# A two-layer MLP on split fp32: the scheme of seven for one more pair of chunks, other staging, output sums in two groups

## Chip, cores and metric

One core of a Trainium2 chip. The metric is the device time of one execution of the whole program in microseconds. An execution of the same program under the profiler gives the trace.

## What is computed

The reference takes x of 2 x 3008 x 256, applies a spectral layer (a Fourier transform along the sequence, a complex 256 x 256 product, soft thresholding, the inverse transform) and then two MLP layers on the 6016 tokens:

```python
h = x @ w_in                                  # 256 -> 2048
x = (h * sigmoid(1.702 * h)) @ w_out          # layer 0, 2048 -> 256
h = x @ w_in2
x = (h * sigmoid(h)) @ w_out2                 # layer 1
```

Only layer 1 and the preparation of its weights during layer 0 are touched by the change. The inputs and outputs are fp32.

## The kernel before, in words

Tokens lie along the free dimension, features along the 128 partitions. The tokens are cut into six blocks; blocks 0 to 4 have two halves of 512 tokens, block 5 has two halves of 448. The 2048 hidden features are cut into eight pairs p of two chunks of 128. A **stage** (l, i, p) is layer l, block i, pair p: its products from x to the hidden features, their activation, and the products to the output. Every fp32 operand is split into a high part and a low part, and one block product is three matmuls (high x high, high x low, low x high).

The products from x to the hidden features of a stage are 2 x 2 blocks, made with seven block products and sums on the operands (`prod`, 21 matmuls). The products to the output are made one stage later than the stage whose factors they use: the standard way with eight block products, 24 matmuls (`out_mm` in layer 0, `out7` in layer 1, called through a list `pend`), or with a scheme of seven block products, 21 matmuls (`s_prod`, called through `S`). `seven(i)` lists the p that use the scheme of seven in layer 1: 1 to 5. Stages with p from 1 to 6 of layer 1 run through `group7`, all others through `group`. In `group7` the factors of a g7 stage are: y1 (factor 1), y4 (2), b22 (3), t1 (5), t2 (6), t3 (7), t4 (4), where t1 = y3 - y1, t3 = b22 - y3, t2 = b22 - t1, t4 = t2 - y4. ScalarE gates and rounds the high parts, GpSimd and VectorE subtract the low parts (`rest`, L1208). The low part of factor 3 is made by ScalarE's negative copy and an accumulating DMA from GpSimd's queue (L1251) that reads b22; the gate of b22 in the next stage overwrites b22.

Sums of products stay in PSUM banks m1, m2, m6, m7 and m3 over a block (`banks`), those of factors 4 and 5 are added into SBUF by VectorE (`accs`). In p = 6 these are combined (`ends`) in u1, u2, a5, a6, and after p = 7 four sums `final` add a bank and an SBUF part, and SyncE copies the result out (L1160, L1162). The weights of the scheme of seven are sums and splits that are made during layer 0 (`stage`, six steps at places given by STEPS, or LATE in block 5), written to DRAM, and loaded in layer 1 by `stream` into the two slots of `ring`, 1 MB a stage. Before that each unit of layer 1's weights is converted from 64-bit input during layer 0 (`window`, in the order of WEIGHTS) and written to DRAM. `halve` stages the weights of the two pairs that stay standard.

The order of all instructions on each engine is that of the program: the regions of the MLP are scheduled by hand, and `hook(h)` marks eight places in a stage at which side work is put in. `xsums`, `xfifth` and `xprep` make the seven operands of the next block from its x (L883, L884, L888, L898, L905). ScalarE copies y1, y2 and y3 out of PSUM, VectorE adds the second product; a product that accumulates on a bank (`first=False`) waits until that copy is done.

The lines the text refers to: L1009 and L1191 products from x, L968 and L1150 standard products to the output, L1127 products of the scheme of seven, L1039 and L1219 first add of a stage, L1069, L1074, L1244, L1246 second and third add, L272 low split in `stage`, L1286 two sums in p = 7, L1110 load of the ring.

Of the kernel before, what the change touches and what calls it, by code (L numbers as in the profile page):

```python
# [34 lines left out]
WEIGHTS += [(kind, 1, p, False) for kind in ("in", "out") for p in range(8)]  # L35
# [21 lines left out]
def spectral_mlp_kernel(ctx, tc, xin, mfwd, minv, wc, bias, w_in1, w_out1, w_in2, w_out2, outT):  # L57
# [938 lines left out]
    def group(l, i, p, hook):  # L996
# [37 lines left out]
        (nc.vector.tensor_copy if (l, i, p) == (1, 0, 0) else nc.scalar.copy)(y1, X)  # L1034
# [142 lines left out]
    def group7(i, p, hook):  # L1177
# [37 lines left out]
        nc.scalar.copy(y1, X)  # L1215
# [9 lines left out]
        if ends:  # L1225
            u1, u2 = (home[x][:, :n] for x in ("b22", "u"))
# [34 lines left out]
        gate(y3)  # L1261
# [13 lines left out]
        if ends:  # L1275
            add(a6, a6, a5)
            add(a5, u2, a5)
            if R3 == 1:
# [7 lines left out]
            steps7.setdefault((1, i, NPR - 1, 5), []).append(lambda: (add(a6, u2, a6), sub(u2, u2, a4)))  # L1286
# [29 lines left out]
    moves[0, last, 3].append(("out", 1, 0))  # L1316
# [284 lines left out]
```

## Time and profile before

| | us |
|---|---|
| median of 3 runs | 1124.08 (1123.69 to 1126.19) |
| profiled execution | 1127.38 |
| its span, first to last instruction | 1125.6 |

The spectral part takes the first 169 us of the span; layer 0 runs from there to 653, layer 1 to the end. A stage begins with the first matmul of its first product. The page of the profile gives the busy time of the engines, a chain of waits and the costliest groups of instructions; the trace behind it answers by stretch, by engine and by line. Stages in the tables are cut at the starts of their first matmuls.

### The profile page before, as it was taken

To read this page: it belongs to the slowest core of one execution; us is meant where nothing else is said; L and a number is where in the kernel's file an instruction comes from. 1 tells how busy PE (TensorE), PEld (TensorE's weight loads), DVE (VectorE), ACT (ScalarE), POOL (GpSimd) and SP (SyncE) were. 2 spreads that over 40 slices of the span, in tenths; PEclk is the share of its full clock that TensorE was granted. 3 is DMA by queue.
4 is the path that set the end of the run, shared out by engine and by line. 5 is a ranking of instruction groups with operands and counts; after the bars stand their busy time and mean duration, and the time that the engine had idled before them with its cause. 6 is when DMAs were issued, how large, how long until landed. Compare 5 with 4: busy or idle time off the path is not lost.

```text
span 1125.6 us, 15165 instructions
## 1 busy us (share of the span) xinstructions
PE 1117.2 (99%) x5000; PEld 928.7 (83%) x5000; DVE 839.8 (75%) x1264; ACT 831.2 (74%) x1567; POOL 584.4 (52%) x491
## 2 busy tenths in 40 slices
PE   9999999999999999999999999999999999999998
PEld 6878987888888888888889888888888888788897
DVE  8779997775575576676577687777877877878776
ACT  2488367776676677676777788878888788697785
POOL 0244056444443444434446638657657567477485
PEclk9999999999999999999999999999999999999999
DMA  8699586531121222312424263145054044242341
GB/s 334 167 169 210 151 155 121 120 73 38 38 75 38 54 60 80 108 48 84 122 94 133 84 233 100 50 160 140 10 192 117 19 151 103 74 142 57 121 138 41
DMA packets 54624, 123.87 MB, mean 110 GB/s; under 512 B 5265, under 2 KB 18193, under 8 KB 50578
## 3 DMA queue, kind: packets, MB, share of 16 engines
q1 hardware_dynamic: 36466, 92.44, 23.1%
q0 software_dynamic: 18080, 30.47, 16.9%
q8 instruction: 39, 0.64, 0.2%
q14 instruction: 39, 0.32, 0.1%
HBM read 71.85 MB, written 20.58 MB: 82 GB/s over the span
## 4 chain that ended last, share of the span: by engine, by line
PE 84%; DVE 7%; DMA 3%; issue 3%; ACT 2%; POOL 1%; SPq 0%; DVEq 0%; POOLq 0%; ACTq 0%
PE x L1009 24%; PE o L968 22%; PE x L1191 13%; PE m L1127 9%; PE m L1150 8%; PE r L1127 3%; PE y L1191 2%; PE psf L448 1%; DMA xl<-xt 1%; DMA x<-yt 1%; DMA xr<-in_x 1%; DMA cv_a<-cv_c 1%; PE psm L642 1%; PE psm L645 1%; POOL xl L567 0%
## 5 line engine op out<-in xcount | busy, mean ns | idle before, releaser
L1022 POOL TENSOR_TENSOR g<-yt,g 128x512 fp32r<-128x512 f32 (+1 forms) x174 | 234.1, 1348 | 274.4 <-PE x L1009 134.9
L1009 PE MATMUL x<-x,wi 128*128 128x512 f32 (+1 forms) x1260 | 314.8, 388 | 2.4 <-ACT yt L1059 2.3
L968 PE MATMUL o<-g,wo 128*128 128x512 f32 (+1 forms) x1152 | 280.3, 385 | 0.0
L1009 PEld LDWEIGHTS x<-x,wi 128*128 128x128 f32 x1260 | 235.3, 188 | 51.9 <-ACT yt L1059 4.9
L968 PEld LDWEIGHTS o<-g,wo 128*128 128x128 f32 x1152 | 216.3, 188 | 40.6
L1208 POOL TENSOR_TENSOR g<-yt,g 128x512 fp32r<-128x512 f32 (+1 forms) x138 | 189.4, 1388 | 74.0 <-ACT g L1204 66.5
L1012 ACT ACTIVATE yt<-yt 128x512 f32<-128x512 f32 (+1 forms) x180 | 112.0, 622 | 142.4 <-DVE yt L1069 114.5
L1191 PE MATMUL x<-x,wi 128*128 128x512 f32 (+1 forms) x648 | 167.9, 385 | 0.1
L1017 ACT CAST g<-yt 128x512 fp32r<-128x512 f32 (+1 forms) x234 | 144.0, 616 | 6.0
L1191 PEld LDWEIGHTS x<-x,wi 128*128 128x128 f32 x648 | 121.5, 188 | 23.2 <-ACT yt L1230 0.6
L1127 PE MATMUL m<-g,ring 128*128 128x512 f32 (+1 forms) x414 | 111.7, 385 | 0.0
L1204 ACT CAST g<-yt 128x512 fp32r<-128x512 f32 (+1 forms) x186 | 107.9, 613 | 4.3 <-DVE yt L1266 1.2
L1150 PE MATMUL m<-g,wo 128*128 128x512 f32 (+1 forms) x396 | 98.0, 386 | 0.0
L188 POOL DMA_DIRECT2D cv_a<-cv_c x32 | 29.7, 928 | 126.6 <-DVE cv_c L187 107.6
L1127 PEld LDWEIGHTS m<-g,ring 128*128 128x128 f32 x414 | 77.7, 188 | 14.6
L1150 PEld LDWEIGHTS m<-g,wo 128*128 128x128 f32 x396 | 74.3, 188 | 14.1 <-POOL g L1022 0.2
L1201 ACT ACTIVATE yt<-yt 128x512 f32<-128x512 f32 (+1 forms) x108 | 67.0, 621 | 21.1 <-DVE yt L1244 17.0
L1069 DVE TENSOR_TENSOR yt<-yt,x 128x512 f32<-128x512 f32 (+1 forms) x60 | 40.4, 673 | 45.7 <-PE x L1009 42.3
L1039 DVE TENSOR_TENSOR yt<-yt,x 128x512 f32<-128x512 f32 (+1 forms) x60 | 40.3, 672 | 41.0 <-ACT yt L1034 40.9
L905 DVE TENSOR_TENSOR x<-yt,x 128x512 fp32r<-128x512 f32 (+1 forms) x55 | 47.2, 858 | 28.9 <-ACT x L898 28.8
L1022 DVE TENSOR_TENSOR g<-yt,g 128x512 fp32r<-128x512 f32 (+1 forms) x60 | 42.2, 704 | 31.7 <-ACT g L1017 31.7
L1133 DVE TENSOR_TENSOR raw<-raw,r 128x512 f32<-128x512 f32 (+1 forms) x48 | 32.4, 675 | 31.5 <-PE r L1127 31.5
(207 smaller groups left out, 1843.9 us busy)
## 6 DMA issues: line engine op xcount, KB each, us to landing
ring<-sout SPq DMA_DIRECT2D x30, 1024.0 KB, 6.2
raw<-in_wi SPq DMA_DIRECT2D x32, 256.0 KB, 3.7
cv_a<-cv_c POOLq DMA_DIRECT2D x32, 256.0 KB, 5.0
raw<-in_wo SPq DMA_DIRECT2D x16, 512.0 KB, 3.8
xl<-xt POOLq DMA_DIRECT2D x22, 256.0 KB, 7.1
out_t<-yt SPq DMA_DIRECT2D x20, 256.0 KB, 2.1
raw<-in_x SPq DMA_DIRECT2D x9, 512.0 KB, 6.3
ge<-yt POOLq DMA_DIRECT2D x15, 256.0 KB, 4.0
```

The source lines that it names most:

```text
L905: E('xl1' if l else 'xl0' if i == 0 else 'xl', k).tensor_sub(lo, src, r32(hi))
L968: nc.tensor.matmul(acc[h, mm], st, mv, start=first and k == 0, stop=last and k == 2)
L1009: nc.tensor.matmul(ps, st, mv, start=first and m == 0, stop=m == 2, skip_group_check=True)
L1012: nc.scalar.activation(g, g if src is None else src, func)
L1017: nc.scalar.copy(gh, g)
L1022: eng.tensor_sub(gl, g, r32(gh))
L1127: nc.tensor.matmul(t, st, mv, start=m == 0 and (one or first and k not in (2, 3)), stop=m == 2, skip_group_check=True)
L1150: nc.tensor.matmul(t, st, mv, start=first and k == 0, stop=k == 2, skip_group_check=True)
L1191: nc.tensor.matmul(ps, st, mv, start=first and m == 0, stop=m == 2, skip_group_check=True)
L1201: nc.scalar.activation(g, g if src is None else src, AF.Silu)
L1204: nc.scalar.copy(factor(i, p, k)[0], src)
L1208: eng.tensor_sub(lo, src, r32(hi))
```

## The change

Seven things are done. `seven` becomes p = 0 to 5, so p = 0 of each block of layer 1 runs through `group7` and makes its output products with `s_prod` in p = 1; the banks are now taken there, and the negative copies that `out7` made for the accumulators go. The unit ("out", 1, 0) is staged like the others, `ring` is allocated in the last stage of layer 0, and the load for p = 0 is queued at step 5 of the stage before. The order of conversion puts the units to be staged first, staging begins in block 2, and in block 5 two units are staged instead of three. `xsums` of layer 1 moves from p = 1 on VectorE to p = 6 on GpSimd. The combination in p = 6 has one accumulator less (a6), and u1 has a place of its own. The four output sums are put between the steps of p = 0 one by one, the last into p = 1. In p = 0 the gate of y3 comes earlier, t2 is made by GpSimd, with the accumulating DMA of factor 3 behind it, and the rounding of t2 goes to p = 1.

```diff
-WEIGHTS += [(kind, 1, p, False) for kind in ("in", "out") for p in range(8)]
+WEIGHTS += [("in", 1, 6, False), ("in", 1, 7, False)] + [("out", 1, p, False) for p in range(6)]
+WEIGHTS += [("in", 1, 0, False), ("in", 1, 1, False), ("out", 1, 6, False), ("out", 1, 7, False)] + [("in", 1, p, False) for p in range(2, 6)]
...
-                t["s"], t[1] = spots(3)[:2]
+                t["s"], t[1] = (tmp()[:, :] if p == 4 else spots(3)[0]), spots(3)[1]
...
-    def xsums(l, i):
+    def xsums(l, i, eng=nc.vector):
...
+                if (mm, h, i + 1) == (1, 0, len(blocks)):
+                    finals.append(lambda y=y, t=acc[h, mm]: nc.vector.tensor_copy(y, t))
+                    continue
...
-        return range(1, NPR - 2)
+        return range(NPR - 2)
...
-    STAGED = {(3, 1): ("in", 6), (3, 3): ("in", 7), (4, 1): ("out", 1), (4, 3): ("out", 2), (5, 1): ("out", 3), (5, 3): ("out", 4), (5, 5): ("out", 5)}
-    LATE = ((0, 1), (0, 4), (1, 3), (1, 4), (1, 3), (1, 5))
-    HALVED = ((0, 1), (0, 4), (0, 5))
+    STAGED = {(2, 1): ("in", 6), (2, 3): ("in", 7), (3, 1): ("out", 0), (3, 3): ("out", 1), (4, 1): ("out", 2), (4, 3): ("out", 3), (5, 0): ("out", 4), (5, 3): ("out", 5)}
+    LATE = ((0, 1), (0, 4), (1, 1), (1, 2), (1, 1), (1, 4))
+    HALVED = ((1, 1), (2, 1), (2, 2))
...
+        if first and not one:
+            banks[k] = ps_p[0].tile([P, 512], F32, tag="D", name="m3") if k == 3 else bank(1, f"m{k}")
...
-        if p == 0 and row != h:
-            t = banks[C_BANK[h, 1]][:, :n]
-            if h:
-                nc.vector.tensor_copy(accs[6][:, :n], t)
-            else:
-                nc.scalar.mul(accs[4][:, :n], t, -1.0)
...
-        nc.scalar.copy(y1, X)
+        (nc.vector.tensor_copy if (i, p) == (0, 0) else nc.scalar.copy)(y1, X)
...
+        if p == 0:
+            gate(y3)
+            while len(finals) > 1:
+                finals.pop(0)()
         rounding(3, b22)
         if g7:
             nc.scalar.mul(factor(i, p, 3)[1], b22, -1.0)
-            nc.gpsimd.dma_start(out=factor(i, p, 3)[1], in_=b22, accum_op=ALU.add)
+            if p:
+                nc.gpsimd.dma_start(out=factor(i, p, 3)[1], in_=b22, accum_op=ALU.add)
...
             nc.vector.tensor_sub(t1, y3, y1)
+            if len(finals) > 1:
+                finals.pop()()
             nc.vector.tensor_sub(t3, b22, y3)
-            nc.vector.tensor_sub(t2, b22, t1)
+            (nc.vector if p else nc.gpsimd).tensor_sub(t2, b22, t1)
+            if not p:
+                nc.gpsimd.dma_start(out=factor(i, p, 3)[1], in_=b22, accum_op=ALU.add)
...
-            add(a6, a6, a5)
             add(a5, u2, a5)
...
+            add(c22, a5, banks[7][:, :n])
             add(u2, u2, banks[7][:, :n])
...
-            steps7.setdefault((1, i, NPR - 1, 5), []).append(lambda: (add(a6, u2, a6), sub(u2, u2, a4)))
+            steps7.setdefault((1, i, NPR - 1, 5), []).append(lambda: sub(u2, u2, a4))
...
+                if k == 6 and p == 0:
+                    later.append(lambda: (rounding(6, t2), rest(nc.gpsimd, 6, t2)))
+                    continue
...
             rest(nc.vector, 2, y4)
+            if finals:
+                finals.pop()()
             after.append(lambda: nc.vector.tensor_sub(home["t4"][:, :n], t2, y4))
+            after.extend(finals)
+            finals[:] = []
...
-    moves[0, last, 3].append(("out", 1, 0))
...
-            steps7.setdefault((0, last, u + q, h), []).append(f)
+            steps7.setdefault((0, last, 2 * u + q, h), []).append(f)
...
+            if h == 5 and more and nxt[0]:
+                stream(nxt[1], 0)
...
-                for x in ({1: (4,), 2: (6,), 3: (5,)} if (l, i) == (1, 0) else {1: (4,), 3: (6, 5)}).get(h, ()):
+                for x in ({1: (4,), 2: (6,), 3: (5,)} if l else {1: (4,), 3: (6, 5)}).get(h, ()):
...
-            if h == (4 if l == 0 and i in (0, last - 1, last) else 1) and p == (NPR - 2 if l == 0 else 1) and (l, i) != (1, last):
-                xsums(*nxt)
+            if h == (5 if l else 4 if i in (0, last - 1, last) else 1) and p == NPR - 2 and (l, i) != (1, last):
+                xsums(*nxt, nc.gpsimd if l else nc.vector)
...
-        if l and 0 < p < NPR - 1:
+        if l and p < NPR - 1:
             group7(i, p, hook)
```

## Rows read from the trace of the kernel before

**Rows 1.** The page: span, TensorE's busy time (share, instructions), granted clock in 40 slices.
```profile
span 1125.6 us, 15165 instructions
...
PE 1117.2 (99%) x5000; PEld 928.7 (83%) x5000; DVE 839.8 (75%) x1264; ACT 831.2 (74%) x1567; POOL 584.4 (52%) x491
...
PEclk9999999999999999999999999999999999999999
```

**Rows 2.** Chain that ended last, 560 us to end: start, us, what.
```profile
604.95 1.82 PE x L1009 x9
...
632.78 1.86 PE x L1009 x9
...
645.52 1.64 DVE yt L272
...
838.74 1.36 PE m L1127 x6
```

**Rows 3.** Stages: us; PE, PEld, DVE, ACT, POOL busy (count); clock; DMA share; GB/s.
```profile
614.51:623.94 9.43, 9.43 (x46) 8.37 (x45) 6.38 (x13) 7.28 (x16) 5.68 (x6) 1.00 0.08 30
623.94:633.24 9.30, 9.30 (x46) 8.45 (x45) 6.63 (x11) 6.63 (x14) 7.17 (x6) 1.00 0.39 141
642.54:652.99 10.45, 9.54 (x47) 8.37 (x46) 9.08 (x13) 6.87 (x15) 4.36 (x3) 1.00 0.63 214
652.99:662.99 10.00, 10.00 (x46) 8.29 (x45) 9.22 (x13) 7.74 (x14) 4.11 (x3) 1.00 0.85 355
...
731.18:741.85 10.67, 10.64 (x46) 8.29 (x45) 8.71 (x13) 8.02 (x16) 4.75 (x3) 1.00 0.01 2
809.85:820.22 10.37, 10.37 (x46) 8.37 (x45) 8.55 (x12) 7.72 (x15) 4.75 (x3) 1.00 0.01 2
820.22:830.42 10.20, 10.20 (x46) 8.45 (x45) 7.79 (x12) 7.81 (x15) 5.30 (x4) 1.00 0.92 331
830.42:839.94 9.52, 9.52 (x43) 7.89 (x42) 7.21 (x11) 8.80 (x17) 7.35 (x6) 1.00 0.37 115
...
946.87:956.83 9.96, 9.84 (x43) 7.80 (x42) 8.28 (x11) 9.38 (x18) 7.76 (x7) 1.00 0.15 26
...
1046.19:1056.10 9.91, 9.91 (x47) 8.37 (x45) 8.35 (x12) 7.43 (x15) 4.55 (x3) 1.00 0.00 0
```

**Rows 4.** Who waited for whom, weight loads, 731 to 1056 us: total, times, longest.
```profile
PEld x L1009 <- DVE x L905: 1.7, 5, 0.5
```

**Rows 5.** VectorE's timeline, (1,2,0) and (1,2,1): start, us, line, shapes, count, idle before.
```profile
811.67 1.67 DVE L1286 TENSOR_TENSOR yt<-yt,raw 128x512 f32<-128x512 f32 x1
813.26 0.68 DVE L1039 TENSOR_TENSOR yt<-yt,x 128x512 f32<-128x512 f32 x1
813.86 1.19 DVE L905 TENSOR_TENSOR x<-yt,x 128x512 fp32r<-128x512 f32 x1
...
821.03 1.28 DVE L1160 TENSOR_TENSOR yt<-yt,m 128x512 f32<-128x512 f32 x2
...
826.61 0.69 DVE L1244 TENSOR_TENSOR yt<-yt,x 128x512 f32<-128x512 f32 x1 [1.34 <-PE x L1191]
```

**Rows 6.** GpSimd's timeline in (1,2,0).
```profile
811.03 3.46 POOL L1022 TENSOR_TENSOR g<-yt,g 128x512 fp32r<-128x512 f32 x2 [4.63 <-ACT g L1017]
815.38 1.29 POOL L1022 TENSOR_TENSOR g<-yt,g 128x512 fp32r<-128x512 f32 x1 [0.89 <-ACT g L1017]
```

**Rows 7.** DMA issues: count, KB each, median us to landing.
```profile
ring<-sout SPq DMA_DIRECT2D x30, 1024.0 KB, 6.2
...
g<-yt POOLq DMA_DIRECT2D x10, 256.0 KB, 4.0
```

**Rows 8.** ScalarE: y3 copy of (1,1,7), y1 copy of (1,2,1), b22 gate of (1,3,5).
```profile
805.35 0.59 ACT L1059 COPY yt<-x 128x512 f32<-128x512 f32 x1
...
821.66 0.58 ACT L1215 COPY yt<-x 128x512 f32<-128x512 f32 x1
...
944.87 0.63 ACT L1201 ACTIVATE yt<-yt 128x512 f32<-128x512 f32 x1 [1.62 <-DMA g<-yt]
```

More of the change, by code (lines that the diff above doesn't have):

```diff
@@ L878, in xhalves @@
         return [[yt[:, mm, t0 + h * n : t0 + (h + 1) * n] for h in range(2)] for mm in range(2)]
-    def xsums(l, i):
+    def xsums(l, i, eng=nc.vector):
         (b11, b12), (_, b22) = xhalves(i)
         xtmp[0] = t = tmp()[:, : blocks[i][1]]
-        E('xse', 0).tensor_sub(t, b12, b11)
-        E('xse', 1).tensor_sub(b12, b22, b12)
+        eng.tensor_sub(t, b12, b11)
+        eng.tensor_sub(b12, b22, b12)
     def xfifth(l, i, src=None):
@@ L1033, in group @@
         prod(X, 0, 0)
-        (nc.vector.tensor_copy if (l, i, p) == (1, 0, 0) else nc.scalar.copy)(y1, X)
+        nc.scalar.copy(y1, X)
         while put_off:
@@ L1126, in s_prod @@
         for m, (st, mv) in enumerate(((a, hi), (z, hi), (a, lo))):
-            nc.tensor.matmul(t, st, mv, start=m == 0 and (one or first and k not in (2, 3)), stop=m == 2, skip_group_check=True)
+            nc.tensor.matmul(t, st, mv, start=m == 0 and (one or first), stop=m == 2, skip_group_check=True)
         if one:
             acc = accs[k][:, :n]
-            if first and k == 5:
+            if first:
                 nc.vector.tensor_copy(acc, t)
@@ L1141, in out7 @@
         for mm in range(2):
-            if p == 0 and row == h:
-                for k in (C_BANK[h, mm],) + ((7,) if h and mm else ()):
-                    banks[k] = ps_p[0].tile([P, 512], F32, tag="D", name="m3") if k == 3 else bank(1, f"m{k}")
             t = banks[C_BANK[h, mm]][:, :n]
-            first = row == h and (p == 0 or p == tail and mm == 1)
+            first = row == h and p == tail and mm == 1
             a = w[:, 0, c % FS, mm * P : (mm + 1) * P]
@@ L1150, in out7 @@
                 nc.tensor.matmul(t, st, mv, start=first and k == 0, stop=k == 2, skip_group_check=True)
-        if p == 0 and row != h:
-            t = banks[C_BANK[h, 1]][:, :n]
-            if h:
-                nc.vector.tensor_copy(accs[6][:, :n], t)
-            else:
-                nc.scalar.mul(accs[4][:, :n], t, -1.0)
         if p == NPR - 1 and row != h:
+            held = [home[("u1", "u", "w", "c22")[2 * h + mm]][:, :n] for mm in range(2)]
             def final(mm):
                 y = yt[:, mm, t0 + h * n : t0 + (h + 1) * n]
-                nc.vector.tensor_add(y, home[("b22", "u", "w", "c22")[2 * h + mm]][:, :n], banks[C_BANK[h, mm]][:, :n])
+                nc.vector.tensor_add(y, held[mm], banks[C_BANK[h, mm]][:, :n])
                 o = outT[mm * P : (mm + 1) * P, t0 + h * n : t0 + (h + 1) * n]
@@ L1196, in S @@
                     s_prod(i, p - 1, k)
-                elif k in (1, 2, 7, 3):
-                    out7_next()
+                elif k in (1, 2, 7):
+                    out7_next(True)
+                    if k == 2:
+                        out7_next(True)
         def gate(g, src=None):
@@ L1225, in group7 @@
         if ends:
-            u1, u2 = (home[x][:, :n] for x in ("b22", "u"))
+            u1, u2, c22 = (home[x][:, :n] for x in ("u1", "u", "c22"))
         prod(Z, 3, 2)
@@ L1255, in group7 @@
             add, sub = nc.vector.tensor_add, nc.vector.tensor_sub
-            a4, a5, a6 = (accs[k][:, :n] for k in (4, 5, 6))
+            a4, a5 = (accs[k][:, :n] for k in (4, 5))
             add(u2, u1, banks[6][:, :n])
@@ L1260, in group7 @@
             rest(nc.vector, 3, b22, (1, 1))
-        gate(y3)
+        if p:
+            gate(y3)
         hook(7)
@@ L1343, in place_tail @@
         w_out[1, k] = w[:, : 2 * FS * D].rearrange("p (h c d) -> p h c d", h=2, c=FS)
-    for at, f, x in (((1, 0, 2, 2), place_tail, 3), ((0, 5, 0, 2), put_aside, 3), ((0, 5, 7, 2), put_aside, 4), ((1, 0, 0, 2), place, 6), ((1, 0, 1, 2), place, 7), ((1, 1, 2, 3), put_back, 3), ((1, 2, 2, 3), put_back, 4)):
+    for at, f, x in (((1, 0, 2, 2), place_tail, 3), ((0, 5, 0, 2), put_aside, 3), ((0, 5, 7, 2), put_aside, 4), ((1, 0, 0, 2), place, 6), ((1, 0, 1, 2), place, 7), ((1, 1, 3, 3), put_back, 3), ((1, 2, 3, 3), put_back, 4)):
         steps7.setdefault(at, []).append(lambda f=f, x=x: f(x))
@@ L1433, in spectral_mlp_kernel @@
             raw64.extend((r[:, : 2 * CU], r[:, 2 * CU :]))
+        if (l, i, p) == (0, last, NPR - 1):
+            ring[:] = [m_p.tile([P, MW], F32R, tag="m", name="ring")[:, : 2 * FS * D] for _ in range(2)]
         if (l, i, p) == (1, 0, 0):
@@ L1440, in spectral_mlp_kernel @@
             accs[5], accs[4] = raw64
-            ring[:] = [m_p.tile([P, MW], F32R, tag="m", name="ring")[:, : 2 * FS * D] for _ in range(2)][::-1]
-            home.update(zip(("t4", "u", "c22"), spots(3)), w=accs[5])
+            home.update(zip(("t4", "u", "c22", "u1"), spots(3)), w=accs[5])
             home.update(zip(("t1", "t2", "t3", "b22"), spots(4)))
@@ L1446, in spectral_mlp_kernel @@
             gs[4, 0] = gs[4, 1] = [cv_p.tile([P, 2 * CU], F32R, tag=x, name="g4", bufs=1) for x in ("ld", "c")]
-        if (l, i, p) == (1, 1, 1):
-            home.update(zip(("t4", "u", "c22"), spots(0)))
-        if (l, i, p) == (1, 2, 1):
+        if (l, i, p) == (1, 1, 2):
+            home.update(zip(("t4", "u", "c22", "u1"), spots(0)))
+        if (l, i, p) == (1, 2, 2):
             home.update(zip(("t1", "t2", "t3", "b22"), spots(1)))
-        accs[6] = home.get("c22")
-        if l and 0 < p < NPR - 1:
+        if l and p < NPR - 1:
             group7(i, p, hook)
```

2 lines of the change are left out of this document (1 added, 1 removed).

## The prediction, made before the changed kernel ran

> **What bounds the kernel now.** I read the page's engine shares first, then the chain of waits, then a table of busy time by stage, and only then the timelines of single engines. TensorE is busy 99% of the span and its granted clock is full speed (its 2.4 GHz level) throughout [rows 1]; the chain from the last instruction backwards is almost only matmuls that follow each other. So the unit of account is the matmul: six of 512 columns take 1.36 us, 0.2267 each, and nine of 448 columns take 1.82, 0.2027 each [rows 2]. With these two prices every stage of layer 1 can be checked: 45 matmuls of 512 should take 10.20 us and 42 should take 9.52, and the stages p = 1 and p = 2 of block 2 take exactly that [rows 3]. What a stage takes beyond its matmuls is a stall. The stages p = 0 carry 0.47 (block 1, and block 4 about the same), 0.17 (block 2, and block 3 the same) and 0.21 (block 5, whose 21 products have 448 columns and whose 24 of the block before have 512: 9.70 due) [rows 3]; their weight loads wait most for L905, VectorE's low part of an operand, 1.7 us in five waits over these blocks [rows 4]. At the end of layer 0 stage (0,5,4) has 0.31 and (0,5,7) has 1.33 over 9.12 [rows 3]; between them nine matmuls take 1.86 instead of 1.82 [rows 2], which is 0.18 a stage, and (0,5,5) shows just that [rows 3]: after a stall 448-column matmuls can go on at 0.2067.
>
> **Matmuls removed.** In p = 0 of a block the standard scheme makes 8 block products of three passes, 24 matmuls, executed one stage later, in p = 1. The scheme of seven makes 21. Five blocks have 512 columns and one has 448: 15 x 0.2267 + 3 x 0.2027 = 4.01 us. TensorE is the bound in that stage, so all of it lies on the path: **-4.01**.
>
> **Staging in layer 0.** The units that need staging move from seven in blocks 3 to 5 (three of them in block 5) to eight in blocks 2 to 5 (two in block 5, none after p = 4). What that does to (0,5,7) is read from the chain: VectorE runs the low split L272 for 1.64 us at 645.5 [rows 2], the first add of (0,5,7) (L1039) waits behind it, the gate behind that, and TensorE waits for ScalarE's copy. Without it that add starts over 1.6 us earlier, more than the stall of 1.33; next late would be that copy, by this sum 0.3 us or more ahead of its matmul. So (0,5,7) falls from 1.33 to the 0.18 of the slow pitch. The stall in (0,5,4) I leave: three ScalarE casts move ahead of its first gate, VectorE's four small sums before them stay where they are, and the gate starts as late as now. Bounds: all 2.0 us of (0,5,4) to (0,5,7) go, or another 448-column stall in (0,5,1) puts 0.18 on three more stages. **-1.15**. Block 2 gets the staging that block 3 has now without a stall: nothing, as long as VectorE and ScalarE keep the slack they have there. The other order of conversion delivers each unit a block or more ahead of its load: nothing. On SyncE the six new 1 MB loads are queued at step 5 of the stage before, behind at most the output copies; a ring load lands in 6.2 us [rows 7] and has over 10: nothing.
>
> **p = 0 of blocks 1 to 5.** The sixth operand is prepared one hook earlier, ahead of ScalarE's copies of y2 and y3 instead of behind them: the stalls of 0.47, 0.17, 0.17, 0.47 and 0.21 go, **-1.5** (bounds: none or all). It has cover from p = 7 too, where one of the two L1286, the 0.69 us one, is gone; the other, 1.67 [rows 5], stays in front of the first add.
>
> **xsums on GpSimd.** It leaves p = 1, where VectorE spent two operations on it, and becomes two GpSimd subtractions at the end of p = 6, 1.29 each alone and up to 1.73 beside VectorE [rows 6]. Behind them on GpSimd stands the low split of the last factor of p = 6, needed 36 matmuls or 8.2 us into p = 7; two subtractions and itself are 3.9 us after the split of y3, which ends about 1 us into p = 7, so it is ready at 5: nothing. VectorE pays for the company: two-input work from SBUF takes 1.67 and 1.19 us [rows 5] while GpSimd works [rows 6], though an add that reads PSUM takes its 0.68 in the same stretch [rows 5]. Here it hits the low split of factor 3, about +1.0, but that stage also loses an SBUF-only sum (a6 += a5) for one that reads PSUM, about -1.0. Net nothing; bounds -0.1 to +0.4 a block, since in p = 7 of block 1 ScalarE's copy of y3 ends at 805.94 [rows 8] and its matmul comes 30 matmuls after the start, at 799.65 + 6.80: half a microsecond.
>
> **The tail of p = 0 and the head of p = 1.** This is where the added work collides. VectorE's order becomes: y2 and y3 sums, output add, t1, output add, t3, low part of factor 2, output add, then in p = 1 the first add, t4, the last output add. Counted from the start of p = 0 at 0.2267 a matmul, the product that ends y3 is issued by 8.16, and VectorE can read it 0.27 later (in (1,2,1) 27 matmuls end at 826.34 and the add starts at 826.61 [rows 3, 5]); at 0.60 us from one VectorE start to the next [rows 5] the adds end at 9.1 and 9.7, t1 (after the gate of y3) at 10.5, the second output add at 11.1. t3 has two SBUF inputs and meets GpSimd's t2 (10.55 to 11.85); at 1.4 us, between the two such rows [rows 5], it ends near 12.4, the low part at 13.0, the third output add at 13.6, the first add of p = 1 at 14.2. TensorE wants the first bank of the new block at 11.56, the second at 13.60 and the bank of the first add at 14.28. So the second bank is level with its user and the third is 0.1 ahead: a stall between 0 and 0.35 a block, and ScalarE's later gate of b22 (about 0.5 late; a wait of 1.62 for the same gate in (1,3,5) goes with 0.44 more in the next stage, 9.96 for 9.52 [rows 3, 8]) gives at most 0.1 more. ScalarE's y1 copy, 1.44 after the start of p = 1 today [rows 8], goes to about 2.2 and is wanted at 2.72. I take 0.15 for each of five blocks, **+0.75**. In block 0 everything is later: layer 0's outputs are copied there too, VectorE is busy 9.22 of 10.00 us [rows 3], and the y1 copy comes at about 3.1, 0.35 late, the second bank another 0.2; with the stage after I put **+0.9** (bounds 0.2 to 1.5).
>
> In the row of 1.67 us VectorE's subtraction starts at 811.67 inside the first of two GpSimd operations of about 1.73 us, and ends at 813.34, some 0.6 us after that first one [rows 5, 6]: it waits for one operation, then runs at its usual length. The Trainium skill, "SBUF — State Buffer", section "Who interferes with whom", says that a VectorE instruction with two SBUF inputs contends with GpSimd's reads and that the loser is blocked for the whole other instruction. The trace agrees with that; what the rule would make of two GpSimd operations in a row, as xsums are, is rival (d).
>
> The skill's "TensorE: Matmul & The Clock Gate", section "Back-to-back issue gap", gives about 131 ns per matmul of 512 columns in a sustained stream; by that the removed matmuls would be worth about 2.4 us and the forecast would be 1120.7 (estimates from that page). The rows here say 226.7 ns, and the measurement decides.
>
> **Sum.** -4.01 - 1.15 - 1.5 + 0.75 + 0.9 = -5.0 us. The profiled execution of before took 1127.38 us for a span of 1125.6, so it would become 1122.4; it lay 3.3 above the median of the three runs, 1124.08, and the same step from the median gives **1119.1 us**.
>
> **Rivals.** (a) Smooth: the head of p = 1 costs nothing and block 5 of layer 0 runs without any stall: -4.01 - 2.0 - 1.5 + 0.2 = -7.3, 1116.8. For it: margins of p = 1 are level, not short. Against it: block 0 of layer 1. (b) Given back: VectorE is 0.5 us later than reckoned at the end of p = 0 (each meeting with GpSimd costs 0.5 to 1.0 [rows 5]), so the second bank, the first add and the gate of b22 are all late: some 0.6 more in each of six blocks and 0.3 in each p = 7, -5.0 + 3.6 + 1.5 = +0.1 to -2.5, 1121.6 to 1124.2. For it: VectorE has the least slack of the helpers there. (c) Slower: GpSimd's accumulating DMA of factor 3 is now queued behind t2, so it starts about 1.9 us into p = 1, and the gate of b22 in p = 1, which overwrites its source, comes at 6.4. At the 4.0 us of its median [rows 7] it lands just in time. In (1,3,5) the gate waited 1.62 us for such a DMA [rows 8]; were it to take over 7 us in every p = 1, beside output copies and a ring load, each next stage would lose about 2.3 us: 6 x 2.3 - 5.0 = +8.8, 1133. It decides from about 1.2 us lost per block. Against it: the ring load starts 1.4 us after it, and most of these DMAs keep to 4.0. (d) Blocked by xsums: if VectorE gets in only behind both GpSimd subtractions and not between them, its low split of factor 3 ends 1.9 us later than the 1.67 of [rows 5], the first add of p = 7 and ScalarE's copies slip as far, and 1.4 us is left after the half microsecond of slack: five blocks, +7 - 5.0 = +2, 1126. Against it: in [rows 5, 6] it got in after one.
>
> **Chances.** Forecast with its own range 1117.8 to 1120.8: 0.60; (a) 0.15; (b) 0.17; (c) 0.05; (d) 0.03. The range takes in (a) to its centre and most of (b): 1116.9 to 1122.5. About 0.2%, or 2.2 us, is what a measurement of this kernel can tell from no change, so faster begins below 1121.8: forecast, (a) and a third of (b), 0.81; same, most of the rest of (b) and half of (d), 0.12; slower 0.07.
>
> **What would show it.** Right: TensorE has 4982 matmuls; stages p = 1 of layer 1 take 9.5 to 9.9 us instead of 10.20, p = 0 takes 10.20 to 10.25; (0,5,7) takes under 9.4. Wrong: a weight load of p = 1 that waits for VectorE's output add (L1160 of before) or for its first add by over 0.5 us; ScalarE waiting for the DMA of factor 3 in p = 1; a first gate of p = 7 that comes later than now. The forecast fails if p = 1 exceeds 10.1 us in most blocks.

## The result, and the profile after

The changed kernel takes **1133.98 us** (1133.78 to 1134.92, 4 runs) against 1123.88 for the kernel before (4 runs): ratio 1.0091 [1.0079, 1.0104], 10.1 us slower. The forecast was 5.0 us faster. The profiled execution of after took 1134.08 us. Its page, span and busy times, beside [rows 1]:

```profile
span 1132.1 us, 15257 instructions
...
PE 1121.8 (99%) x4982; PEld 922.2 (81%) x4982; DVE 851.0 (75%) x1279; ACT 838.3 (74%) x1585; POOL 627.2 (55%) x524
```

The 18 matmuls are gone (5000 to 4982) and the granted clock is 9 in all forty slices as in [rows 1], and yet TensorE is busy 4.6 us longer. Most of the waits here are too short to leave a hole between matmuls and appear as matmuls that stretch, so busy time hides them. The time of a stage shows them. Stages of after, with the columns of [rows 3]: (0,5,4), (0,5,7), (1,0,1), (1,0,3), (1,2,0), (1,2,1), (1,3,1):

```profile
612.54:621.66 9.12, 9.12 (x47) 8.45 (x45) 7.70 (x15) 8.03 (x17) 5.84 (x5) 1.00 0.50 174
639.90:649.02 9.12, 9.12 (x47) 8.45 (x45) 8.02 (x12) 7.61 (x16) 4.06 (x3) 1.00 0.59 218
658.99:669.38 10.39, 10.25 (x43) 7.61 (x42) 7.40 (x12) 9.76 (x19) 9.25 (x8) 1.00 0.15 25
678.93:690.13 11.20, 10.66 (x43) 7.50 (x42) 7.63 (x11) 10.86 (x21) 7.81 (x6) 1.00 0.41 117
810.26:820.96 10.70, 10.49 (x47) 8.37 (x45) 8.00 (x11) 7.77 (x15) 4.37 (x3) 1.00 0.00 1
820.96:831.46 10.50, 10.14 (x43) 7.70 (x42) 8.92 (x14) 9.88 (x19) 8.94 (x8) 1.00 0.73 226
900.91:912.30 11.39, 10.66 (x43) 7.54 (x42) 9.91 (x13) 9.34 (x18) 8.47 (x7) 1.00 0.65 209
```

At the prices of the prediction (0.2267 and 0.2027 a matmul) p = 1 is due 9.52 and takes 10.50, p = 0 is due 10.20 and takes 10.70, and p = 3 of block 0 takes 1.68 over its 9.52. The same subtraction for every stage from (0,0,1) on, summed by kind of stage, gives the account on which the rest stands. It is in us of stall, from the one profiled execution of each kernel; the rows e1 to e9 are the experiments below:

| kernel | layer 0, blocks 0-4 | block 5 | p = 0 | p = 1 | p = 2-5 | p = 6 | p = 7 | last stage | sum |
|---|---|---|---|---|---|---|---|---|---|
| before | 0.08 | 2.04 | 1.90 | 0.04 | 0 | 0.48 | 0.57 | 3.84 | 8.95 |
| **after** | 0.73 | 0.05 | 2.55 | 6.62 | 4.25 | 1.44 | 2.19 | 4.29 | 22.11 |
| e1, x5 early | 0.04 | 0.05 | 0.19 | 2.83 | 4.35 | 3.20 | 1.99 | 4.42 | 17.07 |
| e2, ring later | 0.05 | 0.05 | 2.09 | 6.46 | 0.29 | 0 | 0.07 | 4.14 | 13.16 |
| e5, both | 0.08 | 0.05 | 0.14 | 2.49 | 0 | 0 | 0.04 | 4.16 | 6.96 |
| e7, e5 with xsums on VectorE | 0.07 | 0.05 | 0.12 | 13.8 | 0.18 | 0 | 0 | 4.15 | 18.37 |
| e8, two places for b22 | 0.05 | 0.05 | 2.34 | 6.46 | 2.88 | 0.70 | 1.44 | 4.15 | 18.07 |
| e4, before with a late DMA | 0.09 | 1.99 | 2.39 | 0.03 | 0.95 | 3.96 | 0.81 | 3.89 | 14.11 |
| e6, before with ring later | 0.09 | 1.66 | 1.11 | 0.04 | 0 | 0 | 0 | 3.84 | 6.74 |
| e3, layer 0 part alone | 0.07 | 0.05 | 1.25 | 0 | 0 | 0.88 | 0.41 | 3.83 | 6.49 |
| e9, e3 with ring later | 0.51 | 0.05 | 0.74 | 0 | 0 | 0 | 0 | 3.84 | 5.14 |

From before to after the stalls grow by 13.16 and the matmuls shrink by 4.01, which is +9.15 of the 10.1 us between the medians; the other 0.9 can't be placed, since one execution of each is profiled and the front of the one of before is 2.6 us longer than that of after ((0,0,1) starts at 179.52 against 176.89). A remainder of the same sign, 0.4 or more, is left between before and each other kernel of the table, so it most likely belongs to that one execution of before. The growth has two parts of nearly the same size: **+6.58 in p = 1**, and **+6.83 in p = 2 to 7**, of which the change touches p = 6 and one sum of p = 7.

The lines of after that the rows below name are: L1190 products from x, L1202 gates, L1216, L1229 and L1231 ScalarE's copies of y1, y2 and y3, L899 and L906 rounding and low split of an operand, L1245 and L1247 the sums of y2 and y3, L1220 the first add of a stage, L1274 t3, L1320 t4, L1026 and L1209 low parts of factors, L1133 products of the scheme of seven, L1257 the accumulating DMA, L1114 the ring load.

Who waited for whom in after (total, times, longest): ScalarE's gate of b22 and y3 copy, then the weight loads of the products from x, which wait for the y1 copy:

```profile
ACT yt L1202 <- DMA ge<-yt: 13.5, 10, 3.3
ACT yt L1202 <- DMA g<-yt: 12.3, 9, 2.2
ACT yt L1231 <- DVE x L906: 4.0, 5, 0.9
...
PEld x L1190 <- ACT yt L1216: 5.1, 9, 0.6
```

The first two rows are the gate of b22 waiting for the accumulating DMA of the stage before: 25.8 us in 19 waits. Before had this for one buffer, in two waits:

```profile
ACT yt L1201 <- DMA g<-yt: 2.7, 2, 1.6
```

**Inside p = 0.** Timelines of (1,2,0) in after, which starts at 810.26: first ScalarE, then VectorE, then GpSimd (start, us, line, what; in brackets the idle time before and what ended it):

```profile
814.32 0.60 ACT L1229 COPY yt<-x 128x512 f32<-128x512 f32 x1
815.70 0.59 ACT L1231 COPY yt<-x 128x512 f32<-128x512 f32 x1 [0.78 <-DVE x L906]
816.18 0.64 ACT L1202 ACTIVATE yt<-yt 128x512 f32<-128x512 f32 x1
...
817.43 0.62 ACT L899 CAST x<-tmp 128x512 fp32r<-128x512 f32 x1
...
823.39 0.58 ACT L1216 COPY yt<-x 128x512 f32<-128x512 f32 x1
```
```profile
814.01 2.20 DVE L906 TENSOR_TENSOR x<-yt,x 128x512 fp32r<-128x512 f32 x2 [0.42 <-ACT x L899]
818.08 1.37 DVE L906 TENSOR_TENSOR x<-tmp,x 128x512 fp32r<-128x512 f32 x1 [1.87 <-ACT x L899]
819.37 0.68 DVE L1245 TENSOR_TENSOR yt<-yt,x 128x512 f32<-128x512 f32 x1
819.97 0.67 DVE L1247 TENSOR_TENSOR yt<-yt,x 128x512 f32<-128x512 f32 x1
...
822.55 1.41 DVE L1274 TENSOR_TENSOR yt<-yt 128x512 f32<-128x512 f32 x1
...
825.08 0.68 DVE L1220 TENSOR_TENSOR yt<-yt,y 128x512 f32<-128x512 f32 x1
```
```profile
811.98 3.08 POOL L1026 TENSOR_TENSOR g<-yt,g 128x512 fp32r<-128x512 f32 x2 [4.33 <-ACT g L1021]
817.60 1.29 POOL L1209 TENSOR_TENSOR g<-yt,g 128x512 fp32r<-128x512 f32 x1 [2.54 <-ACT g L1205]
```

In order: VectorE's two low splits (x4, then x6) take 2.20 instead of 1.3, beside GpSimd's 3.08. ScalarE's y3 copy (L1231) writes the place that x4 is made from, so it waits 0.78 for the first of them, and starts at 815.70, before the pair ends at 816.21. Behind that copy stand, in ScalarE's program order, the gate of y1, its rounding, and only then the rounding of x5 at 817.43. Its low split follows at 818.08 and takes 1.37, since GpSimd works at the same time, and in VectorE's program order that split stands ahead of the sums of y2 and y3. These start at 819.37 and 819.97. The prediction had the sum of y3 start 8.43 into the stage, when its product can be read; it starts at 9.71, 1.3 later. What is queued behind it keeps that delay: the first add of p = 1 ends at 825.76, 15.5 after the start of p = 0 instead of 14.2. ScalarE's y1 copy comes 2.43 into p = 1 (823.39) where before had 1.44 [rows 8] and the prediction about 2.2.

**Between the queues.** The accumulating DMA of factor 3 (GpSimd) and the 1 MB load of the ring (SyncE), first of before, in (1,0,3): when they are issued, and how long each took to land (KB, us):

```profile
691.58 0.85 POOL L1251 DMA_DIRECT2D ge<-yt  x1
692.46 0.32 SPq L1110 DMA_DIRECT2D ring<-sout  x1
```
```profile
ring<-sout SPq DMA_DIRECT2D x1, 1024.0 KB, 5.6
ge<-yt POOLq DMA_DIRECT2D x1, 256.0 KB, 4.0
```

The same two of after, in the same stage:

```profile
690.13 0.86 POOL L1257 DMA_DIRECT2D ge<-yt  x1
690.32 0.32 SPq L1114 DMA_DIRECT2D ring<-sout  x1
```
```profile
ring<-sout SPq DMA_DIRECT2D x1, 1024.0 KB, 5.7
ge<-yt POOLq DMA_DIRECT2D x1, 256.0 KB, 7.2
```

In before GpSimd issues 0.88 us ahead of SyncE, about as long as its issue lasts (0.85), and the 256 KB land in 4.0. In after it is 0.19 ahead, and they land in 7.2, later than the four times larger load. Over the whole kernel the two medians go from 4.0 [rows 7] to 7.1 and 7.2.

### The profile page after: what moved, and what is told of

It reads as the page before. It is cut to its first block, busy times and chain, and to the rows that moved or that the text cites. A ratio compares the mean times of both kernels' runs of the same rounds, so it can differ in the third digit from the quotient of the medians.

```text
span 1132.1 us, 15257 instructions
## 1 busy us (share of the span) xinstructions
PE 1121.8 (99%) x4982; PEld 922.2 (81%) x4982; DVE 851.0 (75%) x1279; ACT 838.3 (74%) x1585; POOL 627.2 (55%) x524
## 4 chain that ended last, share of the span: by engine, by line
PE 82%; DMA 6%; ACT 5%; DVE 4%; issue 2%; POOL 1%; SPq 0%; ACTq 0%; DVEq 0%; POOLq 0%
PE x L1013 21%; PE o L969 21%; PE x L1190 10%; PE m L1133 8%; PE psm L646 5%; PE m L1153 4%; PE psi L449 4%; PE r L1133 3%; PE psf L449 3%; DMA ge<-yt 2%; DMA g<-yt 2%; PE y L1190 2%; ACT yt L1202 1%; PE psf L490 1%; DVE x L906 1%
## 5 line engine op out<-in xcount | busy, mean ns | idle before, releaser
L1026 POOL TENSOR_TENSOR g<-yt,g 128x512 fp32r<-128x512 f32 (+1 forms) x156 | 205.8, 1321 | 233.1 <-PE x L1013 129.7
L1209 POOL TENSOR_TENSOR g<-yt,g 128x512 fp32r<-128x512 f32 (+1 forms) x162 | 226.7, 1419 | 63.2 <-ACT g L1205 57.1
L1013 PEld LDWEIGHTS x<-x,wi 128*128 128x128 f32 x1134 | 211.8, 188 | 45.2 <-ACT yt L1063 2.7
L1190 PE MATMUL x<-x,wi 128*128 128x512 f32 (+1 forms) x756 | 199.6, 390 | 2.8 <-DVE yt L1245 0.9
L1190 PEld LDWEIGHTS x<-x,wi 128*128 128x128 f32 x756 | 139.4, 188 | 37.4 <-ACT yt L1216 5.1
L1133 PE MATMUL m<-g,ring 128*128 128x512 f32 (+1 forms) x504 | 136.1, 386 | 0.0
L1205 ACT CAST g<-yt 128x512 fp32r<-128x512 f32 (+1 forms) x222 | 129.2, 612 | 6.2 <-DVE yt L1275 2.4
L1021 ACT CAST g<-yt 128x512 fp32r<-128x512 f32 (+1 forms) x210 | 129.3, 616 | 5.0
L1133 PEld LDWEIGHTS m<-g,ring 128*128 128x128 f32 x504 | 94.6, 188 | 18.4 <-POOL g L1209 0.4
L1202 ACT ACTIVATE yt<-yt 128x512 f32<-128x512 f32 (+1 forms) x126 | 77.8, 619 | 40.4 <-DMA ge<-yt 13.5
L1043 DVE TENSOR_TENSOR yt<-yt,x 128x512 f32<-128x512 f32 (+1 forms) x54 | 36.3, 672 | 42.0 <-ACT yt L1038 42.0
L906 DVE TENSOR_TENSOR x<-yt,x 128x512 fp32r<-128x512 f32 (+1 forms) x55 | 51.9, 950 | 16.1 <-ACT x L899 16.0
L1153 PE MATMUL m<-g,wo 128*128 128x512 f32 (+1 forms) x252 | 61.9, 385 | 0.0
L1073 DVE TENSOR_TENSOR yt<-yt,x 128x512 f32<-128x512 f32 (+1 forms) x54 | 36.4, 674 | 31.1 <-PE x L1013 30.0
L1026 DVE TENSOR_TENSOR g<-yt,g 128x512 fp32r<-128x512 f32 (+1 forms) x54 | 36.8, 682 | 29.8 <-ACT g L1021 29.8
L1133 PE MATMUL r<-g,ring 128*128 128x512 f32 (+1 forms) x198 | 56.4, 392 | 1.5 <-DVE yt L1220 1.1
```

The source lines that it names most:

```text
L1013: nc.tensor.matmul(ps, st, mv, start=first and m == 0, stop=m == 2, skip_group_check=True)
L1021: nc.scalar.copy(gh, g)
L1026: eng.tensor_sub(gl, g, r32(gh))
L1133: nc.tensor.matmul(t, st, mv, start=m == 0 and (one or first), stop=m == 2, skip_group_check=True)
L1153: nc.tensor.matmul(t, st, mv, start=first and k == 0, stop=k == 2, skip_group_check=True)
L1190: nc.tensor.matmul(ps, st, mv, start=first and m == 0, stop=m == 2, skip_group_check=True)
```

## The experiments

Four theories, the last of them put up after the first four runs (those of x5 early, ring later, before with a late DMA, and layer 0 alone). **A**: only the order in p = 0 is at fault; its late sums make the later gates and DMAs late too. **B**: only the order of the two queues is. **C**: xsums on GpSimd is what makes the stages late. **D**: two separate causes that add, the order in p = 0 for p = 1, and the order of the queues for p = 2 to 7.

**x5 early.** The rounding and low split of the fifth operand move one hook forward, ahead of the y2 and y3 copies.

```
-for x in ({1: (4,), 2: (6,), 3: (5,)} if l else {1: (4,), 3: (6, 5)}).get(h, ()):
+for x in ({1: (4,), 2: (6, 5)} if l else {1: (4,), 3: (6, 5)}).get(h, ()):
```

> The changed kernel with one move: in p = 0 of layer 1 the operand of the last product (x5) is rounded at step 2, ahead of ScalarE's copies of y2 and y3, instead of at step 3 behind the gate of y1. Theory A (late sums): the loss begins in p = 0, where the y3 copy waits for VectorE's low part of x4, the gate and x5's rounding queue behind it, x5's low part meets GpSimd, and VectorE's sums y2 and y3 come 1.4 us late; all later losses follow from that. Then p = 0 of blocks 1 to 5 falls from 10.70 to about 10.2 (2.2 us in all), p = 1 from 10.5 to 9.8 or less (3.5 us or more), and most accumulating DMAs of factor 3 land in 4 us again instead of 7.3 (up to 4 us in p = 2 to 6): 1124 to 1127. Rival B (the DMA order alone costs it, whatever p = 0 does): only p = 0 gains, 1131 to 1132. Rival C (xsums on GpSimd costs it): 1132 to 1134.

Measured 1130.62 us, ratio to before 1.0049 [1.0027, 1.0071], which is in none of the three ranges. The stalls of p = 0 go (2.55 to 0.19) and those of p = 1 fall by 3.8, to 2.83. Those of p = 2 to 7 don't fall (7.88 to 9.54), and ScalarE still waits 14.5 and 12.6 us for the two DMA buffers. Theory A falls: the DMAs are late by themselves. The largest part of the 2.83, 1.17, is in one block, 10.69 in (1,3,1). VectorE's t4 there, and the GpSimd operations beside it:

```profile
903.20 2.23 DVE L1320 TENSOR_TENSOR yt<-yt 128x512 f32<-128x512 f32 x1
```
```profile
902.15 2.71 POOL L1209 TENSOR_TENSOR g<-yt,g 128x512 fp32r<-128x512 f32 x2
```

The VectorE operation, 0.79 in (1,2,1) of after, starts inside the first of two GpSimd subtractions and ends at 905.43, 0.57 after the end of the second: it was shut out by both. This is the mechanism of rival (d), at another place. It agrees with the Trainium skill, "SBUF — State Buffer", section "Who interferes with whom", by which the loser is blocked for the whole instruction, and shows that it can lose twice in a row. Why it happens in block 3 alone was not settled.

**Ring later.** SyncE is held in p = 2 to 5 by a copy of 512 bytes that reads factor 5, ahead of the ring load; so the load is issued behind the accumulating DMA. The load for p = 1 is issued in p = 0.

```
+held_up = dram_p.tile([1, P], F32, name="held_up")
...
-if l == 1 and h == 5 and p + 1 in seven(i):
-    stream(i, p + 1)
+if l == 1 and h == 5 and p == 0:
+    stream(i, 1)
+if l == 1 and h == 1 and p > 1 and p in seven(i):
+    nc.sync.dma_start(out=held_up, in_=r32(factor(i, p - 1, 5)[0])[0:1, :P])
+    stream(i, p)
```

> The changed kernel, but the 1 MB ring loads for p = 2 to 5 are held in SyncE's queue until factor 5 of the stage before has been rounded, about 2.1 us into a stage instead of at its start, so that they start behind the accumulating DMA of factor 3. Theory A says that this DMA, once late, falls behind the ring load, lands after 7.3 us, delays the gate of b22 and by it the next such DMA: held back, ScalarE no longer waits for it, p = 2 to 6 give back some 4 us, p = 1 keeps its 10.5: 1129 to 1131. If the wait costs nothing by itself, 1133 to 1134. If rival B holds in full, p = 1 falls too: under 1127.

Measured 1125.41 us, ratio 1.0013 [1.0003, 1.0022]. The same pair of issues as above in this kernel:

```profile
686.50 0.87 POOL L1257 DMA_DIRECT2D ge<-yt  x1
689.26 0.24 SPq L1410 DMA_DIRECT2D held_up<-g  x1
689.59 0.33 SPq L1114 DMA_DIRECT2D ring<-sout  x1
```
```profile
ge<-yt POOLq DMA_DIRECT2D x1, 256.0 KB, 3.3
```

The accumulating DMA is 3.1 us ahead and lands in 3.3, no gate waits for one any more, and the stalls of p = 2 to 7 go from 7.88 to 0.36. The time lies in the range that was given to theory B in full, but not in its way, which had p = 1 fall: p = 0 and p = 1 stay (2.09, 6.46), and p = 2 to 7 give back 7.5 where some 4 was expected. Theory B alone falls too; the two causes are separate.

**Both.** The two edits together.

> The changed kernel with both moves of the first two runs: x5 rounded at step 2 of p = 0, and the ring loads of p = 2 to 5 held behind the accumulating DMA. Theory D (two separate causes that add: late sums in p = 0 and 1, and a DMA order that keeps itself late): stalls of p = 0 near 0.2, of p = 1 near 2.8, of p = 2 to 7 near 0.5 in all: 1119 to 1121, below both kernels. Rival (one cause seen twice): not below 1124.

Measured **1118.86 us** (1118.34 to 1119.5), ratio 0.9955 [0.994, 0.997]: faster than both kernels, 15.1 us below after. Stages (1,2,0), (1,2,1) and (1,3,1) of this kernel:

```profile
803.65:813.86 10.21, 10.21 (x47) 8.45 (x46) 8.03 (x12) 8.53 (x17) 4.38 (x3) 1.00 0.01 2
813.86:823.60 9.74, 9.74 (x44) 7.80 (x43) 8.26 (x13) 9.12 (x18) 8.94 (x8) 1.00 0.78 242
...
891.60:902.55 10.95, 10.40 (x44) 7.60 (x42) 9.55 (x12) 8.91 (x17) 8.51 (x8) 1.00 0.68 217
```

p = 0 is at its 10.20, and p = 1 is 0.22 over its 9.52 (0.30 in block 0, and 1.43 in block 3, where t4 is again shut out by two GpSimd operations and takes 2.21). VectorE in (1,2,0), from 803.65:

```profile
809.48 0.68 DVE L906 TENSOR_TENSOR x<-tmp,x 128x512 fp32r<-128x512 f32 x1
811.40 0.69 DVE L1245 TENSOR_TENSOR yt<-yt,x 128x512 f32<-128x512 f32 x1 [1.25 <-PE x L1190]
812.09 0.69 DVE L1247 TENSOR_TENSOR yt<-yt,x 128x512 f32<-128x512 f32 x1
...
817.21 0.68 DVE L1220 TENSOR_TENSOR yt<-yt,y 128x512 f32<-128x512 f32 x1
```

The split of x5 takes 0.68 again, and the sum of y2 starts 7.75 into the stage, after waiting 1.25 for its product: it is the product that comes last. The sum of y3 starts at 8.44 for the 8.43 of the prediction, and the first add of p = 1 ends at 817.88, 14.2 after the start of p = 0, as predicted. Theory D holds.

**Before with a late DMA.** The converse of ring later: the kernel before, with the low part of y1 in p = 2 subtracted twice on GpSimd (same values), ahead of the negative copy and the DMA. One operation of some 1.3 us [rows 6] more in each block.

```
 if g7:
+    if p == 2:
+        rest(nc.gpsimd, 1, y1)
     nc.scalar.mul(factor(i, p, 3)[1], b22, -1.0)
```

> The kernel before, but in p = 2 of each block of layer 1 GpSimd makes the low part of factor 1 twice (same result), which puts its accumulating DMA of factor 3 about 1.3 us later, just behind SyncE's ring load instead of 0.9 us ahead. Theory A (a late DMA keeps itself late): the DMAs of p = 2, 3 and 4 take over 7 us, the gates of p = 3 to 5 wait 1 to 2 us, and each block loses 0.5 to 1.3 us: 1127 to 1132. Rival: the next stage recovers, 1124 to 1125.5.

Measured 1131.32 us (1128.98 to 1132.9), ratio 1.006 [1.0043, 1.0077]. Issues and landing in (1,0,3), where nothing was added, and ScalarE's waits over the kernel:

```profile
688.67 0.87 POOL L1253 DMA_DIRECT2D ge<-yt  x1
688.90 0.32 SPq L1110 DMA_DIRECT2D ring<-sout  x1
```
```profile
ge<-yt POOLq DMA_DIRECT2D x1, 256.0 KB, 7.2
```
```profile
ACT yt L1201 <- DMA g<-yt: 11.3, 12, 2.4
ACT yt L1201 <- DMA ge<-yt: 7.6, 6, 1.6
```

The addition is in p = 2; the DMA of p = 3 is as late as in after, and the next one, of p = 4, took 7.51. So the late order **keeps itself**: a DMA that lands late holds the gate of b22 in the next stage, that gate holds the next negative copy, and the next accumulating DMA is issued when the slot of the ring comes free, level with the load. Six operations, some 8 us of work on an engine that is busy half the time [rows 1], cost 7.3 us of the kernel by the medians. Most of the stall comes out at the end of the chain, in p = 6. (The profiled execution is the fastest of this kernel, so the table shows less of it, 5.2.)

**Two places for b22.** To cut that chain at its other end: after, with b22 in odd p of blocks 3 to 5 at another place, so that its gate needn't wait for the DMA of the stage before. Blocks 0 to 2 are unchanged.

```
 if not g7:
     b22 = y2
+elif i > 2 and p % 2:
+    b22 = spots(2)[0][:, :n]
```

> The changed kernel, but in blocks 3 to 5 the stages with odd p keep b22 in another place, so that the gate of b22 no longer overwrites what the accumulating DMA still reads; the ring loads are where the change has them. Theory D, with the gate's wait as the way by which a late DMA costs time: in blocks 3 to 5 ScalarE waits for no such DMA, the DMAs land in 3 to 5 us again, and the stalls of p = 2 to 7 there, some 2.8 us, go; blocks 0 to 2 stay: about 1131. Rival (the late low part of factor 3 itself holds up TensorE): blocks 3 to 5 keep their stalls, 1134.

Only one execution was timed, 1129.45 us beside 1123.94 for before. In blocks 3 to 5 no stage of p = 2 to 7 is more than 0.02 over its due (the last stage aside), and the median of `g<-yt` falls to 4.0; in blocks 0 to 2 the stalls stay. In blocks 3 to 5 the DMA of p = 1 is still late (6.9 to 7.6), but those of p = 3 to 5 land in 3.7 to 4.0. So the wait of the gate is what carries the lateness from stage to stage.

**Before with the ring later.** The hold of the second experiment in the kernel before.

```
+held_up = dram_p.tile([1, P], F32, name="held_up")
...
-if l == 1 and h == 5 and p + 1 in seven(i):
-    stream(i, p + 1)
+if l == 1 and h == 5 and p == 0:
+    stream(i, 1)
+if l == 1 and h == 1 and p > 1 and p in seven(i):
+    nc.sync.dma_start(out=held_up, in_=r32(factor(i, p - 1, 5)[0])[0:1, :P])
+    stream(i, p)
```

> The kernel before with the ring loads of p = 2 to 5 held in the same way. Theory D: the few late DMAs of before go, and with them the stalls of p = 6 and p = 7 (1.0 us), little else: 1122.5 to 1123.8. Rival (the later loads help in some other way, through the memory or the weights): 1121 or less, or slower than before if the loads are too late.

Measured 1122.47 us, ratio 0.9989 [0.998, 0.9999]; the medians of the accumulating DMAs go from 4.0 to 3.3, the stalls of p = 6 and 7 (1.05) go, and those of p = 0 fall by 0.8. The kernel before lost about 1.2 us, by the ratio (0.1 to 2.2 by its interval), to the same order; [rows 8], 1.62 for one gate, was a sign of it.

**xsums back on VectorE.** The kernel with both edits, with xsums in p = 1 on VectorE as in before.

```
-if h == (5 if l else 4 if i in (0, last - 1, last) else 1) and p == NPR - 2 and (l, i) != (1, last):
-    xsums(*nxt, nc.gpsimd if l else nc.vector)
+if h == (4 if l == 0 and i in (0, last - 1, last) else 1) and p == (NPR - 2 if l == 0 else 1) and (l, i) != (1, last):
+    xsums(*nxt)
```

> The kernel of both moves with xsums back on VectorE in p = 1, where it was before the change. Theory D: p = 1 is where VectorE has least slack, two operations of 0.68 and 0.68 to 1.67 there make p = 1 and p = 2 longer by 0.3 to 0.8 a block: 1121 to 1125, while p = 6 and 7 don't change. Rival C (xsums on GpSimd is what costs): p = 7 loses its stalls, below the run of both moves by 1 or more.

Measured 1130.93 us, ratio 1.0066 [1.0049, 1.0083], 12 us slower than with xsums on GpSimd. p = 6 and p = 7 stay at 0, as they are in the kernel with both edits (0.04), so the two GpSimd subtractions cost nothing there: theory C falls. In p = 1, where VectorE has no room, they cost 11.3, far more than the 0.3 to 0.8 a block that was expected. Stages (1,1,1) and (1,3,1), then the second in pieces of 2 us from 904; behind them TensorE's wait for VectorE's copy of an accumulator:

```profile
737.99:749.73 11.74, 10.02 (x43) 7.73 (x42) 10.53 (x14) 8.85 (x18) 9.98 (x8) 1.00 0.66 202
897.74:911.80 14.06, 11.39 (x44) 8.73 (x43) 12.77 (x17) 9.92 (x19) 10.15 (x8) 0.89 0.55 172
...
904.00:906.00 2.00, 0.87 (x4) 0.38 (x2) 1.97 (x3) 1.97 (x4) 1.35 (x1) 1.00 1.01 393
906.00:908.00 2.00, 0.46 (x2) 0.45 (x3) 2.00 (x4) 0.27 (x1) 2.00 (x3) 1.00 0.52 197
908.00:910.00 2.00, 2.00 (x8) 1.59 (x7) 1.20 (x2) 1.95 (x4) 1.18 (x1) 0.68 0.03 8
910.00:912.00 2.00, 2.00 (x6) 1.53 (x5) 1.54 (x3) 1.46 (x3) 0.88 (x1) 0.50 0.25 43
```
```profile
PE r L1133 <- DVE raw L1137: 9.8, 5, 2.7
```

**Layer 0 alone.** The kernel before with the conversion order and the staging of the change (WEIGHTS, LATE and HALVED as there), with seven units instead of eight.

```
-STAGED = {(3, 1): ("in", 6), (3, 3): ("in", 7), (4, 1): ("out", 1), (4, 3): ("out", 2), (5, 1): ("out", 3), (5, 3): ("out", 4), (5, 5): ("out", 5)}
+STAGED = {(2, 1): ("in", 6), (2, 3): ("in", 7), (3, 3): ("out", 1), (4, 1): ("out", 2), (4, 3): ("out", 3), (5, 0): ("out", 4), (5, 3): ("out", 5)}
...
```

> The kernel before with the layer 0 part of the change alone: the other order of conversion, seven units staged in blocks 2 to 5, two of them in block 5, the halves later; layer 1 as before. All theories: (0,5,4) to (0,5,7) lose 2.0 us of stalls, (0,4,4) may gain up to 0.65: 1121.5 to 1123.2.

Measured 1122.01 us, ratio 0.9977 [0.9966, 0.9987]. Block 5 of layer 0 loses its stall wholly (2.04 to 0.05).

**Without the scheme for p = 0.** The layer 0 part and the hold (the two diffs above), on the kernel before.

> The kernel before with the layer 0 part of the change and the ring loads held: everything that gains, without the scheme of seven for p = 0. If the scheme is worth its 4.0 us less the 2.5 of stalls that are left in p = 1, this lies about 1.5 to 3 us above the run of both moves: 1120.3 to 1122. If the gain of that run came from the order of the DMAs and layer 0 alone, it equals it: 1118.5 to 1119.5.

Measured 1120.83 us, ratio 0.9974 [0.9963, 0.9984]. Against 1118.86 with all of it, the scheme of seven for p = 0 brings 2.0 of its 4.01 us. The intervals of the two ratios touch, so 2.0 is rough, but the table gives about the same: 4.01 less the 1.82 by which its stalls are more (6.96 for 5.14), above all the 2.49 in p = 1.

## Why the prediction was wrong

- **Matmuls removed, -4.01**: right, 4982 are left.
- **Staging in layer 0, -1.15**: too small. All 2.0 went, since the stall of (0,5,4), which I left standing, went too (9.12 for 9.43), and with it the slow pitch after it. The 0.65 that after has more in blocks 0 to 4 is mostly (0,4,4), 10.77; the other kernels with this staging have at most 0.25 there.
- **p = 0, -1.5**: wrong sign, +0.65. Not all of the old stall was the sixth operand's, either: holding the ring loads alone took 0.8 of it away in the kernel before. I followed the sixth operand, which did move ahead of the copies, and not the fifth. x5 is now rounded behind the y3 copy and the gate of y1, and x4's split holds that copy. In before the same rounding stood behind the y3 copy as well, but the gate of y1 was ahead of both copies and the sums were not pressed.
- **Tail of p = 0 and head of p = 1, +0.75 and +0.9**: the step that failed is its first one, that the adds end at 9.1 and 9.7 because the sum of y3 starts as soon as its product can be read, at 8.43. It started at 9.71, 1.3 later, and the first add of p = 1 ended 1.3 later; the margins there were 0 and 0.1, as I had worked out, so most of it came out: 0.9 to 1.0 a block, 1.9 in block 3, 6.6 in all. With the sums on time the same working holds, in the kernel with both edits: the sum of y3 at 8.44, the first add at 14.2, 0.22 measured a block for 0.15, and 0.30 in block 0, under my 0.9. What it lacked is t4 shut out by two GpSimd operations in block 3, 1.4 us.
- **Ring loads, "nothing"**: the second step that failed, worth +6.83. I checked that a load has time to land and not whom it delays, and beside the loads I counted SyncE's output copies only; the queue that matters is GpSimd's, whose DMA of p = 1 is now issued level with a ring load (in block 0 of before it met none and landed in 3.3), in the stage in which GpSimd has most to do (8 operations, 8.94 us).
- **Rival (c)** had the size (1133) and the mechanism, a gate of b22 held by an accumulating DMA that takes over 7 us, with the chance 0.05. But the DMA that it named, that of p = 0, lands in 3.3 to 3.5, and it is those of p = 1 to 5 that are late (9.2, 4.8, 7.2, 7.3 and 7.5 in block 0); and the cause is not the queue behind t2 but the order against the ring load. I had the sign in [rows 8] and read it as a single accident; the one at p = 4 of block 0, 7.6 us, stood in the same trace.
- **Rival (b)**, VectorE half a microsecond late, is what p = 1 shows; I priced the gate of b22 in it at 0.3 a p = 7, not as a chain.
- **xsums, 0**: right. **Rival (d)**: not there, but the same mechanism in p = 1 of block 3.
- **The signs**: p = 1 over 10.1 us was named as the sign of failure, and is what came. The wait of ScalarE for the DMA of factor 3 came too, one stage later than I had looked for it.

That the kernel with both edits lies at the forecast, 1118.86 for 1119.1, is partly chance: it gains the 1.2 us of the hold and 0.85 more in layer 0, which the forecast did not have, and loses 1.4 in block 3, which the forecast did not have either.

## What to carry to other kernels

When a step is moved, list every operand that the helper engine makes in that stretch and follow the one that ends up last in each engine's program order; a margin of zero behind it turns any lateness into the same lateness on the path. A transfer is priced twice: by when it lands, and by which other transfer it now meets, and a small one that overwrites or frees a buffer once a stage should be issued clearly ahead of a large one. If its landing holds its own successor, one late start costs every stage that follows.

## What the runs showed of the hardware

- In the pairs of (1,0,3) shown above, a 256 KB accumulating DMA from GpSimd's queue lands in 3.3 us when the 1 MB load from SyncE's queue is issued 3.1 us behind it, in 4.0 when 0.88 behind, and in 7.2 when 0.19 or 0.23 behind. In block 0 of before it took 4.0 at 0.84 and 0.88, and 7.6 at 0.90. The edge may lie near the length of GpSimd's own issue (0.85); these few cases don't settle it.
- A VectorE operation with two SBUF inputs takes 0.69 alone, 1.37 and 1.41 beside one GpSimd operation, and 2.23 beside two in a row.
- In the kernel with xsums back on VectorE, TensorE waits 2.7 us in (1,3,1), to 907.54, and behind that its granted clock falls to the 1.2 GHz level: 1.00 from 906 to 908, a mean of 0.68 from 908 to 910, 0.50 from 910 to 912. A stage of 9.52 takes 14.06, of which 2.7 are the wait; the lower clock costs 1.6 more by these two rows (2 us at 0.68 and 2 at 0.50 are worth 2.36 at full speed). In (1,1,1), where the same wait is 1.72, the clock stays at 1.00.
